# A decode step with all its gradients: turned weights as the stationary side of the output-gradient products

## The chip, the cores and the metric

The kernel runs on one core of a Trainium2 chip. The metric is the device time of one execution in microseconds (us). Five engines share the work: TensorE (PE in the profile; its weight loads are PEld), VectorE (DVE), ScalarE (ACT), GpSimd (POOL) and SyncE (SP), which issues nearly all DMAs.

## The reference

A forward pass and the gradients of all its inputs but one are wanted. B = 2 rows of width 576 are normalized to xn, and

```
out = x + A(xn) + M(xn)
A:  q = xn wq (32 heads of 128);  scores q k / sqrt(128) over 4096 cached positions (16 kv heads, 2 q heads each);
    p = softmax;  o = p v;  A = o wo
M:  g = xn w_gate, u = xn w_up (576 -> 4608);  h = g u;  M = h w_down
outputs: out, and for grad_out = dy the gradients of x, k_cache, v_cache, wq, wo, w_gate, w_up, w_down
```

All data are bf16. The caches (2 x 16 x 4096 x 128 each, 33.5 MB) are read once and their gradients, of the same size, are written once; so are the weights and theirs. The profile counts 92.48 MB read and 92.48 MB written.

The weight gradients are outer products of two rows each: of wo it is o (4096 long, called R in a group of 512) times dy; of w_down it is h (4608 long, called hb in a block of 512) times dy; of w_gate and w_up it is xn times the gradients of g and u (D in the code). The products that need dy from the left are dy wo^T (the gradient of o) and dy w_down^T (the gradient of h).

## The kernel before

**Pieces.** Attention goes in 8 groups of 4 q heads (2 kv heads), each for 2 batch rows, so 16 steps. `group_front` makes q and the gradient of o for a group, `softmax` and `dscore` the scores of a step and their gradients, `contract` (matmuls at L1378) the two context products, `head_outer` (L1226) the cache gradients as outer products, `group_back` what follows on o and q. The MLP goes in 9 blocks of 512 columns, `mlp`, loaded in pairs.

**Turning.** A product that contracts over a weight's or cache's free dimension needs it turned. DVE turns 32x32 blocks of pairs of bf16 (as fp32), in `t32` (L418), into a buffer X. So after a turn, the two elements of a pair stay side by side, and products take every second element: index e or parity in the code.

**Output-gradient products.** In `group_front` (L967) and `mlp` (L841), dy, laid out in `Wdy` with zeros around, is the stationary side (128x128) and the turned weights X the moving side, 128 columns; 18 products add up 576 rows. The result in PSUM has a batch row for each 32-block of partitions. In `group_front` it is copied to `dof`, turned on PE (L978) and copied to qd; in `mlp` it is multiplied with gs into D (L849).

**Row products of weight gradients.** `rows_outer` makes a 512x576 gradient of wo or w_down as 4 units (`rows_unit`). A unit is 8 matmuls at L675 with 32 contracted rows and a stationary side of 32 columns: for each of 2 banks, four matmuls that stand on the diagonal of the array (rows 32q, output partitions 32q). The result is evicted as 2 x 288 columns into a staging buffer, and `put` (L644) stores it.

**Evictions and buffers.** `cp` copies on ACT (L422) or DVE (L424). PSUM has three double banks `ps_o` for what is evicted to staging, and two banks `ps_m` for everything else, which a stream holds from ACQ("m") to REL("m"). 16 buffers of 1 MB ("big") hold cache tiles, turned tiles and staging; a cache load waits for a free one.

**What sets the order.** Each piece is a generator that yields what it needs (an engine with a cost, a buffer, an event). A planner (`Order`) runs when the program is built: it keeps a clock for each engine by the yielded costs, a line for the DMAs, and picks what starts first, by priorities in the table PRI and a slack for each engine; `BIAS` weighs DVE against ACT for evictions, and `AT` says after which cache load a weight load may be issued. So the order of every engine's instructions, and that of SP's DMA queue, comes from these numbers. On the chip each engine follows that order and waits for semaphores. Engines issue in order: behind a waiting instruction everything on its engine waits.

## Time and profile before

| | |
|---|---|
| time, median of 3 runs | 472.86 us (472.06 to 473.0) |
| profiled execution | 471.37 us, its span 469.6 us |
| mean granted PE clock | 0.71 |
| busy PE / PEld / DVE / ACT / POOL | 370.8 / 217.5 / 369.5 / 334.3 / 146.8 us |
| moved | 185.96 MB, 396 GB/s over the span |
| PE matmuls | 6636 |

The span runs from the first to the last instruction of the profiled execution. Busy times are of that execution; overlapping matmuls of a group count once. The strip of the profile cuts the span into 40 equal slices and gives each engine's busy tenths, the granted clock of TensorE in tenths, the share in which the DMA engines were busy, and the rate. A group's row names line, engine, operation, tiles and shape, then the busy time of the whole group, the mean duration of one instruction in ns, and the idle time of the engine before them with what ended it.

### The profile page before, as it was taken

Reading aid. Unit: us, or ns where it says so; the run is one execution under the profiler, and the core shown is the slowest. Engines: PE = TensorE matmul, PEld = TensorE weight load, DVE = VectorE, ACT = ScalarE, POOL = GpSimd, SP = SyncE. Lnnn points to the kernel's source line nnn. Section 1 sums busy time; section 2 is a strip of 40 time slices with the busy share of each in tenths; the row PEclk is TensorE's granted clock in tenths of the full one; section 3 lists DMA queues with packets and bytes.
Section 4 is the critical chain, followed back from the end, with each engine's and each line's share of the span. In section 5 each row is a group of like instructions: output and inputs, shape, how many; then the busy total and the mean of one; then the engine's idle time right before and its main releaser. Section 6 shows DMA issues by size and latency. Waiting matters only on the chain.

```text
span 469.6 us, 15459 instructions
## 1 busy us (share of the span) xinstructions
PE 370.8 (79%) x6636; PEld 217.5 (46%) x6636; DVE 369.5 (79%) x705; ACT 334.3 (71%) x507; POOL 146.8 (31%) x176
## 2 busy tenths in 40 slices
PE   0588688869887777986997669789699898998984
PEld 0455444435653352554463444564345434444453
DVE  9689878967867879688689658978867978898772
ACT  2149668867885948671798638877678678789973
POOL 3350242681330320203252264000843705325100
PEclk9978897767757668776675767956656658566977
DMA  8999999999999999999999999999999989999995
GB/s 317 404 413 403 363 390 419 409 416 421 418 416 420 399 421 406 412 415 419 399 418 404 386 418 424 408 413 342 413 416 393 424 270 416 423 413 413 424 368 176
DMA packets 40053, 185.96 MB, mean 396 GB/s; under 512 B 3496, under 2 KB 11184, under 8 KB 23600
## 3 DMA queue, kind: packets, MB, share of 16 engines
q1 hardware_dynamic: 39976, 184.96, 98.1%
q8 instruction: 52, 0.85, 0.7%
q14 instruction: 17, 0.14, 0.1%
q10 hardware_dynamic: 8, 0.00, 0.0%
HBM read 92.48 MB, written 92.48 MB: 394 GB/s over the span
## 4 chain that ended last, share of the span: by engine, by line
PE 42%; ACT 18%; DVE 18%; DMA 12%; issue 5%; POOL 2%; SPq 2%; ACTq 0%; DVEq 0%; POOLq 0%
ACT big L422 15%; DMA out_dram<-big 10%; DVE big L418 8%; PE ps_m L1378 8%; PE ps_o L1226 7%; PE ps_m L1205 7%; PE ps_o L675 4%; PE ps_m L841 3%; DVE big L424 3%; DMA big<-in_A_v_cache_dram 3%; PE ps_m L967 2%; PE ps_m L636 2%; POOL BD L1193 2%; PE ps_o L712 1%; SPq L1129 1%
## 5 line engine op out<-in xcount | busy, mean ns | idle before, releaser
L422 ACT CAST big<-ps_o 128x1024 bf16<-128x1024 f32 (+4 forms) x319 | 279.7, 950 | 40.3 <-PE ps_o L1226 18.2
L418 DVE STREAM_TRANSPOSE big<-big 128x1024 f32<-128x1024 f32 x146 | 176.1, 1223 | 5.9 <-DMA big<-in_A_v_cache_dram 3.6
L1193 POOL TENSOR_TENSOR BD<-vr,mask 128x2048 bf16<-128x2048 bf16 x32 | 115.2, 3603 | 198.8 <-ACT vr L422 122.2
L424 DVE CAST big<-ps_o 128x1024 bf16<-128x1024 f32 (+2 forms) x71 | 78.2, 1102 | 15.8 <-PE ps_o L675 5.2
L1205 PE MATMUL ps_m<-big,W 128*32 128x128 bf16 x2048 | 57.1, 274 | 5.5 <-ACT osb L422 0.7
L1226 PE MATMUL ps_o<-BD,dd 32*128 32x512 bf16 x256 | 48.8, 489 | 12.7 <-ACT big L422 9.2
L1205 PEld LDWEIGHTS <-W 128*32 128x32 bf16 x2048 | 45.4, 121 | 21.9 <-issue 18.6
L1226 PE MATMUL ps_o<-BD,pp 32*128 32x512 bf16 x256 | 42.1, 461 | 10.4 <-ACT big L422 6.7
L1170 POOL COPY W<-rep 32x16 bf16<-32x16 bf16 x128 | 24.5, 192 | 63.5 <-DVE rep L951 53.2
L418 DVE STREAM_TRANSPOSE big<-ww 128x1152 f32<-128x1152 f32 (+1 forms) x25 | 32.9, 1317 | 4.5 <-DMA out_dram<-big 3.3
L1378 PE MATMUL ps_m<-big,pp 128*32 128x512 bf16 x256 | 28.2, 536 | 1.5 <-DVE small L1330 1.2
L1378 PE MATMUL ps_m<-big,dd 128*32 128x512 bf16 x256 | 27.5, 518 | 1.5 <-DVE dd L418 0.6
L1226 PEld LDWEIGHTS <-dd 32*128 32x128 bf16 x256 | 11.8, 97 | 32.4 <-issue 24.7
L1226 PEld LDWEIGHTS <-pp 32*128 32x128 bf16 x256 | 10.4, 95 | 26.9 <-issue 22.6
L422 ACT CAST osb<-ps_m 128x512 bf16<-128x512 f32 x15 | 8.9, 590 | 15.9 <-PE ps_m L1378 12.6
L675 PE MATMUL ps_o<-dyr,R 32*32 32x288 bf16 x256 | 17.3, 402 | 2.0 <-ACT big L422 2.0
L675 PE MATMUL ps_o<-dyr,hb 32*32 32x288 bf16 x288 | 16.5, 346 | 1.1 <-ACT big L422 0.9
L967 PE MATMUL ps_m<-big,Wdy 128*128 128x128 bf16 x144 | 14.9, 285 | 3.1 <-DVE small L1283 2.0
L712 PEld LDWEIGHTS <-xnr 32*128 32x128 bf16 x368 | 12.5, 119 | 9.3 <-issue 8.6
L422 ACT CAST sp<-ps_m 128x256 bf16<-128x256 f32 x22 | 8.4, 380 | 11.2 <-PE ps_m L1213 11.0
L636 PEld LDWEIGHTS <-wm 128*32 128x32 bf16 x704 | 13.4, 115 | 6.3 <-issue 5.1
L841 PE MATMUL ps_m<-big,Wdy 128*128 128x128 bf16 x162 | 15.6, 272 | 0.6 <-DVE small L1291 0.4
(210 smaller groups left out, 481.9 us busy)
## 6 DMA issues: line engine op xcount, KB each, us to landing
out_dram<-big SPq DMA_DIRECT2D x74, 1024.0 KB, 12.1
big<-in_A_k_cache_dram SPq DMA_DIRECT2D x32, 1024.0 KB, 12.4
big<-in_A_v_cache_dram SPq DMA_DIRECT2D x32, 1024.0 KB, 12.5
out_dram<-big SPq DMA_DIRECT2D x17, 576.0 KB, 11.4
ww<-in_B_w_down_dram SPq DMA_DIRECT2D x9, 576.0 KB, 11.1
ww<-in_A_wo_dram SPq DMA_DIRECT2D x8, 576.0 KB, 11.1
ww<-in_A_wq_dram SPq DMA_DIRECT2D x8, 512.0 KB, 11.6
big<-in_B_w_gate_dram SPq DMA_DIRECT2D x4, 1024.0 KB, 13.1
```

Of the source, the lines that this page charges most:

```text
L418: nc.vector.transpose(out, in_)
L422: nc.scalar.copy(out, in_)
L424: nc.vector.tensor_copy(out=out, in_=in_)
L636: nc.tensor.matmul(dp[32 * q:32 * q + 32, :], lhsT=view(Wm[:], 0, P, 8 * pos(q, s), [[1, 32]]), rhs=view(X, 0, P, xoff(q, s), [[FS, blocks ...
L675: nc.tensor.matmul(o[32 * q:32 * q + 32, aa, 0:HD2], lhsT=view(t, 32 * q, 32, 2 * A + aa, [[4, 32]]), rhs=dyr[32 * q:32 * q + 32, k * HD2: ...
L841: nc.tensor.matmul(dh, lhsT=Wdy[:, e, 2 * k:2 * k + P], rhs=view(X[:], 0, P, 64 * k + e, [[D, FC], [2, 32]]), start=(k == 0 and e == 0), s ...
L967: nc.tensor.matmul(dp, lhsT=Wdy[:, e, 2 * k:2 * k + P], rhs=view(X[:], 0, P, 64 * k + e, [[D, GH], [2, 32]]), start=(k == 0 and e == 0), s ...
L1170: nc.gpsimd.tensor_copy(view(W_t[t][w][:], 32 * a, 32, 6 + 8 * a, [[G * WW, 4], [WW, G], [1, 2]]), view(rep_t[grp[g]["qs"]][:], 32 * a, 32 ...
L1193: nc.gpsimd.tensor_tensor(BD_t[i][:], view(vr_t[v][:], 0, P, 0, [[0, 16], [1, Dh]]), view(mask16[:], 0, P, 0, [[1, 16], [0, Dh]]), ALU.mult)
L1205: nc.tensor.matmul(sc[32 * cq:32 * cq + 32, :], lhsT=view(W[:], 0, P, (be * G + l) * WW + 6 - 4 * c2 - 2 * l, [[1, 32]]), rhs=view(X[:], 0 ...
L1226: nc.tensor.matmul(o[:, k, :], lhsT=pr2[32 * c4:32 * c4 + 32, :], rhs=BD[32 * c4:32 * c4 + 32, 8 * l + 4 * h2:8 * l + 4 * h2 + 4, :], star ...
L1378: nc.tensor.matmul(ct[32 * j:32 * j + 32, :], lhsT=view(rT, 0, P, 4 * c + 2 * l, [[1, 32]]), rhs=kv_t[kvS[s][t][l]][:, Dh * c:Dh * (c + 4) ...
```

## The change

**Output-gradient products.** The turn writes X in another order (`turn_rows`), so that 128 columns of one product lie at a step of two elements. X is now the stationary side (128x128), and dy, packed as 8 columns in `dy8`, the moving side (`dy_products`): 18 products again, with 8 moving columns each. The result has the 512 positions on partitions and in 4 columns per batch row. In `group_front` it is copied straight to qd, and `dof` with its transpose goes. In `mlp` it is copied to E, and a product of E with a rearranged identity (`unmix`) gives the gradient of h in the layout that D needs. `selx` and `unmix` serve the changed order of positions where qd is used later.

**Row products.** A unit is now 2 matmuls with 32 contracted rows and a stationary side of 128 columns, one in each of the two banks. For this hb and R hold the positions in the order c, p instead of p, c: `mlp` turns hb by DVE into hT as before (earlier now), transposes hT on PE and copies it back to hb; `group_back` builds R by 16 products with strided columns of the identity instead of 4 transposes. rT comes from a PE transpose and a copy of 8 columns instead of a DVE turn, and gT from two PE transposes and a copy of 16 columns instead of a DVE turn.

**Order.** The MLP row products are spawned before the wait for w_down instead of after D. The costs that the streams yield follow the new pieces, and the numbers in PRI, AT, BIAS and SLACK are other ones, found by a new search.

```diff
--- before.py
+++ after.py
@@ -257 +257 @@
 PRI = {
-    "turn0": [12127.5, 6592.3, 21769.7, -2605.1, ...
+    "turn0": [23153.9, 17883.7, 20715.9, 24467.2, ...
...
 AT = {
-    "wq": [-5, 7, 11, 24, 31, -18, 50, -5],
-    "wo": [-13, -2, -15, 2, 36, -14, 47, 53],
-    "mlp": [2, 16, -13, 39, 111],
+    "wq": [-20, 4, -15, 24, 28, 2, 47, -17],
+    "wo": [-20, -11, -20, 24, 36, -11, -2, -5],
+    "mlp": [2, 15, -12, 39, 86],
 }
@@ -301 +301 @@
 CLK = 1.65
-BIAS = 0.21111771427708687
-SLACK = {"PE": 0.0, "ACT": 0.11786185086953341, "DVE": 0.44815392421950667, "POOL": 1e9, "SP": 1e9}
+BIAS = 0.27538315644118333
+SLACK = {"PE": 0.0, "ACT": 0.03971586105496694, "DVE": 0.4579872161471015, "POOL": 1e9, "SP": 1e9}
 
@@ -380 +380 @@
     hT_t = [const.tile([P, FC, 32], BF16, name=f"hT{i}") for i in range(2)]
-    gT_t = [const.tile([P, 8, 32], BF16, name=f"gT{i}") for i in range(2)]
+    gT_t = [const.tile([P, 4, 2, 2], BF16, name=f"gT{i}") for i in range(2)]
     wm_t = tiles("wm", 2, [P, 35, 8])
@@ -386 +386 @@
     rep_t = [const.tile([P, 2, 4, GH * 2], BF16, name=f"rep{i}") for i in range(2)]
-    dof = const.tile([P, P], BF16, name="dof")
-    rT = const.tile([P, GH, 32], BF16, name="rT")
+    E_t = [const.tile([P, 4, 32], BF16, name=f"E{i}") for i in range(2)]
+    rT = const.tile([P, GH, 2], BF16, name="rT")
     R_t = tiles("R", 2, [P, P])
@@ -454 +454 @@
             nc.gpsimd.memset(t[r], 0.0)
-    Wdy = filled("Wdy", [P, 2, 160], BF16, 0.0)
+    dy8 = filled("dy8", [P, 2 * NB, 4, 2], BF16, 0.0)
     xnd = filled("xnd", [P, 2, P], BF16, 0.0)
@@ -459 +459 @@
 
-    for t in (*W_t[0], *W_t[1], *wm_t, *oT_t):
+    for t in (*W_t[0], *W_t[1], *wm_t, *oT_t, *E_t):
         nc.vector.memset(t[:], 0.0)
@@ -469 +469 @@
     identP = const.tile([P, P], BF16, name="identP")
-    selA = const.tile([P, 4, 4, 32], BF16, name="selA")
+    selx = const.tile([P, 4, 4, 16, 2], BF16, name="selx")
+    unmix = view(ident[:], 0, P, 0, [[1, 32], [32, 4]])
     K4 = const.tile([P, 4], FP32, name="K4")
@@ -514 +515 @@
         for be in range(4):
-            nc.vector.tensor_copy(selA[:, be], view(ident[:], 0, P, 32 * be, [[0, 4], [1, 32]]))
+            nc.vector.tensor_copy(selx[:, be], view(ident[:], 0, P, 32 * (be % 2) + 16 * (be // 2), [[0, 4], [1, 16], [64, 2]]))
         yield DVE(0.2)
@@ -547 +548 @@
         for a in range(4):
-            nc.vector.tensor_copy(
-                view(Wdy[:], 32 * a, 32, 32 * a, [[2, NB], [160, 2], [1, 2]]),
-                dyT[32 * a:32 * a + 32, :, 0:2].rearrange("p (k e) b -> p k e b", e=2))
+            nc.vector.tensor_copy(dy8[32 * a:32 * a + 32, :, a, :], dyT[32 * a:32 * a + 32, :, 0:2])
         yield SET(Edy)
@@ -668 +667 @@
 
+    def dy_products(out, X):
+        for k in range(NB):
+            for e in range(2):
+                nc.tensor.matmul(out, lhsT=view(X[:], 0, P, 2 * P * k + e, [[2, P]]),
+                                 rhs=dy8[:, 2 * k + e].rearrange("p a b -> p (a b)"),
+                                 start=(k == 0 and e == 0), stop=(k == NB - 1 and e == 1))
+
+    def turn_rows(X, w):
+        t32(pairs(X[:, 0:WB]).rearrange("p (k c i) -> p c k i", c=FC, i=32),
+            pairs(w[:]).rearrange("p (c k r) -> p c k r", c=FC, r=32))
+
     def rows_unit(j, t, st):
@@ -673 +683 @@
             for aa in range(2):
-                for q in range(4):
-                    nc.tensor.matmul(o[32 * q:32 * q + 32, aa, 0:HD2], lhsT=view(t, 32 * q, 32, 2 * A + aa, [[4, 32]]),
-                                     rhs=dyr[32 * q:32 * q + 32, k * HD2:(k + 1) * HD2], start=True, stop=True)
+                c = 2 * A + aa
+                nc.tensor.matmul(o[:, aa, 0:HD2], lhsT=t[32 * c:32 * c + 32, :],
+                                 rhs=dyr[32 * c:32 * c + 32, k * HD2:(k + 1) * HD2], start=True, stop=True)
 
@@ -679 +689 @@
             cp(e, view(st[:], 0, P, 2 * A * D + k * HD2, [[D, 2], [1, HD2]]), o[:, :, 0:HD2])
-        return mms, (0.12, 0.208), D, ev
+        return mms, (0.12, 0.052), D, ev
 
@@ -810 +820 @@
         hs = yield ACQ("hb")
-        hb, hT, gT = hb_t[hs], hT_t[hs], gT_t[hs]
-        f0 = i * FS
+        hb, hT, gT, E = hb_t[hs], hT_t[hs], gT_t[hs], E_t[hs]
         yield WAIT(Lgu, Exn, Emore, Ezero)
@@ -828 +837 @@
         nc.vector.tensor_tensor(hb[:], gs[:, 0], ug[:, 1], ALU.mult)
-        yield REL("m", m)
+        yield DVE(0.31)
+        t32(hT[:].rearrange("p c m -> p (c m)"), view(hb[:], 0, P, 0, [[1, 4], [4, 32]]))
+        hp = m_t[m][:].bitcast(BF16)[:, 4 * P:5 * P]
+        yield PE(0.053, 0.03)
+        nc.tensor.transpose(hp, hT[:].rearrange("p c m -> p (c m)"), ident[:])
+        e = yield EV(128)
+        cp(e, hb[:], hp)
+        yield REL("m", m)
+        hE = Event()
+        yield SPAWN(rows_outer(hb[:], out_8[i * FS:(i + 1) * FS, :], pr("mlp", i) + pr("wout"), hE),
+                    pr("mlp", i) + pr("wout"))
 
@@ -834 +853 @@
         yield DVE(1.37)
-        t32(pairs(X[:, 0:FC * D]), pairs(wd[:, 0:FC * D]))
-        m = yield ACQ("m")
+        turn_rows(X, wd)
+        m = yield ACQ("m")
+        dT = m_t[m][:, 2 * P:2 * P + 8]
+        yield PE(0.0, 0.47)
+        dy_products(dT, X)
+        yield REL("X", x)
+        e = yield EV(8)
+        cp(e, E[:, :, 0:2], dT.rearrange("p (a b) -> p a b", b=2))
         dh = m_t[m][:, 0:P]
-        yield PE(0.96, 0.47)
-        for k in range(NB):
-            for e in range(2):
-                nc.tensor.matmul(
-                    dh, lhsT=Wdy[:, e, 2 * k:2 * k + P], rhs=view(X[:], 0, P, 64 * k + e, [[D, FC], [2, 32]]),
-                    start=(k == 0 and e == 0), stop=(k == NB - 1 and e == 1),
-                )
-        yield REL("X", x)
+        yield PE(0.053, 0.03)
+        nc.tensor.matmul(dh, lhsT=E[:].rearrange("p a m -> p (a m)"), rhs=unmix, start=True, stop=True)
         Ds[i] = ds = yield ACQ("D")
@@ -848 +867 @@
         yield DVE(0.42)
-        nc.vector.tensor_tensor(
-            view(D2[:], 0, P, 0, [[P, 2], [4, 32], [1, 4]]), view(dh, 0, P, 0, [[0, 2], [1, 32], [32, 4]]),
-            view(gs[:], 0, P, 0, [[P, 2], [4, 32], [1, 4]]), ALU.mult)
+        nc.vector.tensor_tensor(D2[:], view(dh, 0, P, 0, [[0, 2], [1, P]]), gs[:], ALU.mult)
         yield REL("m", m)
@@ -855 +872 @@
 
-        E = [Event()]
         po = pr("mlp", i) + pr("wout")
-        yield SPAWN(rows_outer(hb[:], out_8[f0:f0 + FS, :], po, E[0]), po)
         for ks in BUNCH:
@@ -861 +876 @@
                 yield SPAWN(grads(ks, po), po)
-        yield DVE(0.31)
-        t32(hT[:].rearrange("p c m -> p (c m)"), view(hb[:], 0, P, 0, [[1, 4], [4, 32]]))
-        yield DVE(0.41)
-        t32(gT[:].rearrange("p c m -> p (c m)"), view(D2[:], 0, P, 0, [[64, 4], [1, 2], [2, 32]]))
+        ws = yield ACQ("wm")
+        m = yield ACQ("m")
+        rp, tp = m_t[m][:, 0:64], m_t[m][:].bitcast(BF16)[:, 4 * P:6 * P]
+        yield PE(0.107, 0.06)
+        for w in range(2):
+            nc.tensor.transpose(tp[:, w * P:w * P + P], D2[:, w], ident[:])
+        e = yield EV(16)
+        cp(e, gT[:], view(tp, 0, P, 0, [[32, 4], [P, 2], [1, 2]]))
         yield SET(dE[i][1])
-
-        ws = yield ACQ("wm")
-        m = yield ACQ("m")
-        rp = m_t[m][:, 0:64].rearrange("p (k b) -> p k b", b=2)
         yield PE(0.0, 0.104)
-        for a in range(4):
-            nc.tensor.matmul(rp[:, 8 * a:8 * a + 8, :], lhsT=selA[:, a].rearrange("p a i -> p (a i)"),
-                             rhs=gT[:, :, 0:2], start=True, stop=True)
+        for be in range(4):
+            nc.tensor.matmul(view(rp, 0, P, 2 * be, [[8, 8], [1, 2]]), lhsT=sel[:, be].rearrange("p a i -> p (a i)"),
+                             rhs=gT[:].rearrange("p a w b -> p (a w) b"), start=True, stop=True)
         yield from stationaries(ws, rp, 32, 0.42)
@@ -914 +929 @@
         yield SET(left[1].pop())
-        yield WAIT(*E)
+        yield WAIT(hE)
         yield REL("hb", hs)
@@ -947 +962 @@
             for be in range(4):
-                nc.tensor.matmul(rp[:, be, :], lhsT=sel[:, be].rearrange("p a i -> p (a i)"),
+                nc.tensor.matmul(rp[:, be, :], lhsT=(sel[:, be].rearrange("p a i -> p (a i)"), selx[:, be].rearrange("p a i e -> p (a i e)"))[t],
                                  rhs=qd[:, t].rearrange("p h b -> p (h b)"), start=True, stop=True)
@@ -960 +975 @@
         yield DVE(1.37)
-        t32(pairs(X[:, 0:GH * D]), pairs(wo[:, 0:GH * D]))
-        m = yield ACQ("m")
-        dp = m_t[m][:, 0:GH * 32]
-        yield PE(0.96, 0.47)
-        for k in range(NB):
-            for e in range(2):
-                nc.tensor.matmul(
-                    dp, lhsT=Wdy[:, e, 2 * k:2 * k + P], rhs=view(X[:], 0, P, 64 * k + e, [[D, GH], [2, 32]]),
-                    start=(k == 0 and e == 0), stop=(k == NB - 1 and e == 1),
-                )
+        turn_rows(X, wo)
+        m = yield ACQ("m")
+        dT = m_t[m][:, 0:8]
+        yield PE(0.0, 0.47)
+        dy_products(dT, X)
         yield REL("X", x)
-        e = yield EV(128)
-        cp(e, view(dof[:], 0, P, 0, [[1, 4], [4, 32]]), dp.rearrange("p (c i) -> p c i", c=4))
-        yield REL("m", m)
-        m = yield ACQ("m")
-        dT = m_t[m][:].bitcast(BF16)[:, 0:P]
-        yield PE(0.0, 0.1)
-        nc.tensor.transpose(dT, dof[:], ident[:])
         e = yield EV(8)
-        cp(e, qd[:, 1], view(dT, 0, P, 0, [[32, GH], [1, 2]]))
+        cp(e, qd[:, 1], dT.rearrange("p (h b) -> p h b", b=2))
         yield REL("m", m)
@@ -996 +999 @@
         m = yield ACQ("m")
-        rp = m_t[m][:].bitcast(BF16)
-        yield PE(0.0, 0.21, kind="c")
-        for t in range(2):
-            for h in range(GH):
-                nc.tensor.transpose(rp[32 * h:32 * h + 32, P * t:P * t + P], oT[:, t, h, :], ident[:])
-        for t, x in ((0, R), (1, Q)):
+        rp, qp, rq = m_t[m][:, 0:P], m_t[m][:].bitcast(BF16)[:, 2 * P:3 * P], m_t[m][:].bitcast(BF16)[:, 3 * P:4 * P]
+        yield PE(0.08, 0.3, kind="c")
+        for h in range(GH):
+            for c in range(4):
+                nc.tensor.matmul(rp[32 * c:32 * c + 32, 32 * h:32 * h + 32], lhsT=oT[:, 0, h, :],
+                                 rhs=view(ident[:], 0, P, c, [[4, 32]]), start=True, stop=True)
+        for h in range(GH):
+            nc.tensor.transpose(qp[32 * h:32 * h + 32, :], oT[:, 1, h, :], ident[:])
+        for x, t in ((R, rp), (Q, qp)):
             e = yield EV(128)
-            cp(e, x[:], rp[:, P * t:P * t + P])
+            cp(e, x[:], t)
+        yield PE(0.053, 0.03)
+        nc.tensor.transpose(rq, R[:], ident[:])
+        e = yield EV(8)
+        cp(e, rT[:], rq.rearrange("p (c m) -> p c m", m=32)[:, :, 0:2])
         yield REL("m", m)
@@ -1007 +1017 @@
         po = pr("back", g) + pr("wout")
-        yield DVE(0.31)
-        t32(rT[:].rearrange("p c m -> p (c m)"), view(R[:], 0, P, 0, [[1, 4], [4, 32]]))
         yield SPAWN(rows_outer(R[:], out_5[n0:n0 + FS, :], po, E[0]), po)
@@ -1186 +1194 @@
                                  lhsT=qr_t[grp[g]["qs"]][:, t, b, :],
-                                 rhs=ident[:], start=True, stop=True)
+                                 rhs=(ident[:], unmix)[t], start=True, stop=True)
                 e = yield EV(128)
```

## The prediction

> **What bounds the kernel now.** I read the page's strip of 40 slices first, then the stretches, the DMA queue's waits, the chain, and last the groups by shape. The strip and the queue table:
>
> ```profile
> PEclk9978897767757668776675767956656658566977
> DMA  8999999999999999999999999999999989999995
> GB/s 317 404 413 403 363 390 419 409 416 421 418 416 420 399 421 406 412 415 419 399 418 404 386 418 424 408 413 342 413 416 393 424 270 416 423 413 413 424 368 176
> ...
> q1 hardware_dynamic: 39976, 184.96, 98.1%
> ```
>
> A slice is 469.6/40 = 11.74 us. A typical undisturbed one moves 415 GB/s, and 185.96 MB at that rate take 448.1 us: the span is 21.4 us longer than its bytes. Slice by slice, (415 - rate)/415 x 11.74 us puts 2.8 us into the first slice (nothing loaded yet), 8.1 us into the last two (the drain), and a net 10.6 us between, of which the slices at 342 and 270 GB/s (from 317 and 376 us) hold 2.1 and 4.1, and those at 363 and 390 (47 to 70 us) 2.2. No edit can win more than about these 21 us, and only what starves the queue can be won. Three stretches (columns: length, busy PE, PEld, DVE, ACT, POOL with counts, granted clock, DMA share, GB/s):
>
> ```profile
> 0.00:20.00 20.00, 4.17 (x77) 2.81 (x81) 17.73 (x78) 5.22 (x9) 5.49 (x13) 1.00 0.92 350
> ...
> 340.00:360.00 20.00, 19.31 (x233) 9.16 (x231) 13.50 (x27) 16.66 (x23) 8.28 (x16) 0.57 1.02 403
> ...
> 455.00:470.00 15.00, 7.29 (x190) 5.13 (x190) 4.92 (x19) 6.40 (x10) 0.00 (x0) 0.73 0.50 177
> ```
>
> And who held SP's queue from 372 to 390 us (us in all, times, longest):
>
> ```profile
> SPq L1087 <- PE ps_m L1378: 7.8, 1, 7.8
> SPq L1087 <- DVE big L418: 5.4, 1, 5.4
> SPq L644 <- DVE big L424: 5.0, 1, 5.0
> ```
>
> In the worst stretch a cache load waited 7.8 us for PE's context products (L1378) to release its buffer, and a store 5.0 us for an eviction. Over the whole span SP waited 112.3 us for ACT's evictions (L422) and 90.6 us for DVE's (L424): the queue is fed just in time by products and evictions together. PE is 370.8 us busy, 79%, and 42% of the chain, with the edited lines on it (L675 3.9%, L841 2.7%, L967 2%). So PE matters, but only through starved stretches. The rows that the edit is priced by (busy us in all, mean ns of one):
>
> ```profile
> L1226 PE MATMUL ps_o<-BD,dd 32*128 32x512 bf16 x256 | 48.8, 489 | 12.7 <-ACT big L422 9.2 <-DVE big L424 1.3 <-POOL BD L1193 0.9
> ...
> L675 PE MATMUL ps_o<-dyr,R 32*32 32x288 bf16 x256 | 17.3, 402 | 2.0 <-ACT big L422 2.0
> L675 PE MATMUL ps_o<-dyr,hb 32*32 32x288 bf16 x288 | 16.5, 346 | 1.1 <-ACT big L422 0.9
> L841 PE MATMUL ps_m<-big,Wdy 128*128 128x128 bf16 x162 | 15.6, 272 | 0.6 <-DVE small L1291 0.4
> L967 PE MATMUL ps_m<-big,Wdy 128*128 128x128 bf16 x144 | 14.9, 285 | 3.1 <-DVE small L1283 2.0 <-DVE small L1330 0.6 <-DVE big L418 0.4
> ...
> L882 PE MATMUL ps_m<-hT,ww 128*128 128x2 bf16 x180 | 5.9, 164 | 0.2 <-DVE oT L1398 0.2
> ```
>
> **Part 1, row products.** 17 blocks (8 of R, 9 of hb) of 4 units. A unit is now 8 matmuls; busy (17.3 + 16.5)/68 = 0.50 us. It becomes two matmuls of the L1226 shape, 288 columns for 512. L1226 with both its operands is 48.8 + 42.1 us for 256 units, 0.355 us; times 288/512 that is 0.20. Saved 0.30 x 68 = 20 us of PE. If the two did not run beside each other in their two banks, 0.40 a unit, 7 us saved; if they were bound by nothing but issue, 0.10, 27 us. I take 20, since L1226 already has this shape and two banks. The evictions stay 576 columns at 651 ns (ACT) or 749 ns (DVE).
>
> **Part 2, output-gradient products.** 17 times 18 matmuls with 128 moving columns, (15.6 + 14.9)/17 = 1.79 us. The same 18 with 8 moving columns and a freshly loaded 128x128 stationary are like L882: 5.9/9 = 0.66 us for 20, so 0.59 for 18. Saved 1.2 x 17 = 20 us. The new stationary is read with a step of two elements; no row has that at 128 columns. From L882's 96 ns to L841's 144 ns median weight load it is 0.59 to 0.9 us, so 15 to 20 us saved; I keep 20, the row with the same moving width.
>
> **Part 3, what is added on PE.** Per MLP block one transpose for hb, one product with unmix for dh, two transposes for gT; per group one for rT, while that of dof goes. By dof's own row (2.0/8 = 0.25 us) 9 x (0.25 + 0.25 + 0.3) + 8 x 0.25 - 2.0 = 7.2 us. R is put together by 16 small products instead of 4 transposes: 8 transposes are 2.7/8 = 0.34 us now, 20 pairs by L882 0.66, so 8 x 0.35 = 2.8 us more. Net PE: -20 - 20 + 10 = -30 us of 371.
>
> **Part 4, DVE and ACT.** Gone: the 32x32 turns into gT (9 x 405 ns) and rT (8 x 306 ns), 6.1 us of DVE, and dof's copies (7 on ACT, 3.2 us, one on DVE). New evictions: hb 9 x 0.28 (the vr copy's row), E, gT and rT 26 x 0.17 (the qd copy's row), 6.9 us shared by both. Net -2.7 us: I take 0. The turn of a weight block keeps its 1152 elements (1361 ns) in another write order. For other orders the trace has 678 ns for 512 elements and 417 for 256, up to 1.63 ns an element: 0 to 0.5 us more, 17 times 0 to 8.8 us. I take 0, the row of the same size, and keep 8.8 for the range. The start-up fills (E for part of Wdy, selx for selA) lie where PE idles: nil, and at most 0.4 us.
>
> **The added waits.** PE's unmix product now waits for E's copy (0.17 us, but behind whatever ACT or DVE is evicting, up to 1.2 us), and behind it on PE stand all later products. In the new PE order other products lie between the two in 8 blocks of 9 (six attention outer products, 0.97 us on the chain, or four fold products, 0.25); in one block nothing does. So the cost is 0 to 9 x 1.2 = 11 us of PE; I take 0.5 us for the open block, which disappears in rounding, and keep the rest for the range. The transposes of rT and hb wait for a copy or a turn in the same way.
>
> **Part 5, what moves.** The MLP row products and their 576 KB stores no longer wait for w_down and dh; ahead of them now stand one DVE turn (291 ns), one transpose and one copy, about 1.2 us with the handoffs, during which one of the two ps_m banks stays taken. Against that the group front drops one bank turn, and its chain from turned wo to qd is shorter by 1.2 + 0.45 + 0.25 us. I set the two equal. All DMAs stay, at other places in SP's queue, since the whole order was drawn again. After the last w_down load 10.9 MB of stores are left instead of 11.9, with an out row again ahead of the last few: the drain keeps its shape.
>
> **The sum.** 30 us less PE work cannot show as 30 us; it shows where the queue starved. From 317 to 329 us six row units lie between the products that stores waited for (0.3 each, 1.8, of which I take -1.5). At the end two runs of L675 with 16 matmuls each (1.15 and 0.98 us) hold the store at 458 us: four units, -1.2. From 47 to 66 us two row units and one L967 run: -1. In the worst stretch no edited line runs; a PE that carries 8% less gets there with less backlog, and I give it half of its 4.1: -2. Together -5.7. The profiled execution took 471.37 us (1.77 beside its span), 1.49 below the median, so 471.37 - 5.7 + 1.49 = 467.2 us. A difference under 0.2% (0.9 us) is about what a measurement of this kernel can't tell from no change.
>
> **The clock.** The rows show no law in busy time: 1.00 where PE was 4.17 of 20 us busy, 0.57 where it was 19.31. At the low clock L841 takes 2.08 us, at the high one 1.21. The Trainium skill (TensorE: Matmul & The Clock Gate, Part 1) says the reverse of those rows: the gate starts throttled, and a busy window releases it. By that rule a lighter PE loses clock. The trace disagrees at both ends, so its chance is small.
>
> **Rivals.** (a) The clock falls with the dense dy products gone. A mean lower by 0.05 means 10% more of the span at half rate: 47 us x 0.79 busy x 0.7 longer = 26 us more PE, which eats the 30. Time then 472 to 473: no change. Against it: the two stretches above. 6%. (b) The queue is full 98.1% of the time and a new order starves it elsewhere by as much: 472 to 473. 6%. (c) Slower, by one mechanism: SP issues in order, so one load placed ahead of ready stores and held for a kv buffer by PE or DVE stops all behind it, as at 370 us (7.8 us waited, 4.1 lost). With two more such places, each 4.1, against -3.7 (the part of the gain that doesn't hang on the worst stretch, which stays) the time is 472.9 + 4.5 = 477.4; one more place takes all of it back. For it: the order is new everywhere and SP stood 16.5 us for L1378. Against: less PE ahead of L1378. 24%. (d) The change doesn't do what it says: the two-bank row products run one after the other, and strided weight loads are slow. Parts 1 and 2 shrink to 7 + 15 us, net 12, two fifths of the gain: 470.6. 10%. (e) Nearly all of the middle is won: -10 to -14, 459 to 463. 14%.
>
> **How the numbers follow.** My forecast (about 464 to 470) has 40%. Faster: 40 + 14 + 10 and a little of (b), 66%; same: 6 + 4 = 10%; slower: 24%. The range leaves out a little at each end: low 458 (case e), high 479 (case c, with some of DVE's 8.8 us). The likeliest sign's own range is 459 to 471.
>
> **What would show it.** Right: L675 at two matmuls a unit and under 0.25 us a unit; the dy products at 0.55 to 0.9 us a run; PE near 340 us busy; mean clock 0.68 to 0.75; fewer slices below 400 GB/s. Wrong: an SP wait of over 5 us for L1378's successor at two or more places, weight-block turns well over 1.36 us, or a PE as busy as before.

## The result, and the profile after

The changed kernel takes 473.85 us (median of 22 runs, 471.77 to 476.27). The kernel before, run as often beside it, takes 471.56 us (469.98 to 474.91), a little less than its three runs above. The ratio is 1.0042, 95% interval 1.0025 to 1.0059: slower by 2.0 us (2.3 by the two medians), where 5.7 us less were forecast. The profiled execution of after took 472.13 us, its span is 470.3 us, and its mean granted clock 0.622 against 0.710. That execution was one of its fastest, so the two spans, only 0.7 us apart, show less than the medians do.

The page of after, the rows that answer to those of before:

```profile
PE 380.9 (81%) x6360; PEld 204.7 (44%) x6360; DVE 372.9 (79%) x723; ACT 330.7 (70%) x501; POOL 146.6 (31%) x176
...
PEclk9999655665556657555665556666656665656655
DMA  8999989999999999999999999999999999999975
GB/s 297 408 406 417 419 307 416 366 414 416 425 421 335 390 413 424 425 414 422 422 418 417 375 415 350 421 420 380 417 418 423 421 423 423 424 418 338 423 310 222
...
q1 hardware_dynamic: 39976, 184.96, 97.9%
```

PE has 276 matmuls fewer and is busy 10.1 us longer. From the fifth slice on the clock's row is fives and sixes but for one seven; before, 22 of the 40 slices had a seven or more. (The nines in front are no full clock; the section on the prediction comes to that.) At 415 GB/s the shortfall is 3.3 us in the first slice, 8.4 in the last two and 10.5 between, against 2.8, 8.1 and 10.6. The hole that was deepest before (270 GB/s, from 376 us) is gone; those at 307 (59 us), 335 (141 us), 350 (282 us) and 338 GB/s (423 us) are new and cost 3.1, 2.3, 1.8 and 2.2 us.

The same stretches as before (length, busy PE, PEld, DVE, ACT, POOL with counts, granted clock, DMA share, GB/s):

```profile
0.00:20.00 20.00, 3.97 (x69) 2.60 (x73) 17.73 (x80) 5.22 (x9) 5.26 (x13) 1.00 0.92 340
...
340.00:360.00 20.00, 19.01 (x264) 8.62 (x264) 16.02 (x32) 18.01 (x24) 10.55 (x19) 0.57 1.01 421
...
455.00:470.00 15.00, 10.93 (x170) 7.39 (x165) 6.86 (x18) 7.54 (x10) 0.00 (x0) 0.50 0.70 261
```

In the first two, PE's busy time and the clock are nearly as they were. In the last one the clock is 0.50, where it was 0.73.

Groups of PE in after (busy us in all, mean ns of one). L1213 is the score product, L1234 the outer product of the caches' gradients, L1386 the context product: the same instructions in the same number as L1205, L1226 and L1378 of before. L685 is the row product, L671 the dy product:

```profile
L1213 PE MATMUL ps_m<-big,W 128*32 128x128 bf16 x2048 | 62.9, 295 | 5.4 <-DVE vr L424 1.0 <-DVE qd L424 0.8 <-DVE qd L952 0.8
L1234 PE MATMUL ps_o<-BD,dd 32*128 32x512 bf16 x256 | 53.6, 519 | 11.1 <-ACT big L422 10.7 <-DVE big L424 0.3
L1234 PE MATMUL ps_o<-BD,pp 32*128 32x512 bf16 x256 | 50.4, 571 | 8.8 <-ACT big L422 4.9 <-POOL BD L1201 3.2
L1386 PE MATMUL ps_m<-big,pp 128*32 128x512 bf16 x256 | 32.8, 619 | 2.4 <-DVE small L1338 1.3 <-DVE pp L418 0.5 <-ACT vr L422 0.4
L1386 PE MATMUL ps_m<-big,dd 128*32 128x512 bf16 x256 | 31.1, 587 | 3.1 <-DVE dd L418 2.0 <-DVE oT L1406 0.3 <-DVE sp L424 0.3
...
L685 PE MATMUL ps_o<-dyr,R 32*128 32x288 bf16 x64 | 11.0, 388 | 1.2 <-ACT big L422 0.8
L685 PE MATMUL ps_o<-dyr,hb 32*128 32x288 bf16 x72 | 11.0, 412 | 1.3 <-ACT big L422 0.8 <-DVE big L424 0.3
L671 PE MATMUL ps_m<-dy,big 128*128 128x8 bf16 x306 | 10.7, 168 | 3.4 <-DVE small L1291 0.8 <-DVE small L1299 0.6 <-DVE big L418 0.5
```

The edited lines shrank: row products from 33.8 to 22.0 us, dy products from 30.5 to 10.7. The five attention groups, in which nothing was edited, grew from 203.7 to 230.8 us; the four of them that the lines above did not show were these:

```profile
L1205 PE MATMUL ps_m<-big,W 128*32 128x128 bf16 x2048 | 57.1, 274 | 5.5 <-ACT osb L422 0.7 <-issue 0.7 <-POOL W L1170 0.7
...
L1226 PE MATMUL ps_o<-BD,pp 32*128 32x512 bf16 x256 | 42.1, 461 | 10.4 <-ACT big L422 6.7 <-POOL BD L1193 2.0 <-DVE big L424 0.7
L1378 PE MATMUL ps_m<-big,pp 128*32 128x512 bf16 x256 | 28.2, 536 | 1.5 <-DVE small L1330 1.2 <-ACT sp L422 0.3
L1378 PE MATMUL ps_m<-big,dd 128*32 128x512 bf16 x256 | 27.5, 518 | 1.5 <-DVE dd L418 0.6 <-DVE small L1283 0.5 <-DVE wm L629 0.2
```

What SP's queue waited for in after, first from 56 to 72 us, then from 280 to 294 us, the longest wait of each (us, times, longest):

```profile
SPq L1095 <- PE ps_m L1386: 6.4, 1, 6.4
```

```profile
SPq L1095 <- PE ps_m L1386: 8.4, 1, 8.4
```

A cache load stands in the queue until the context products release its buffer, and with it all that SP has behind it: two waits of over 5 us, where before had one. The holes at 141 and 423 us have no such wait. From 139 to 156 us SP waited longest for evictions by DVE (5.8 us in 2 waits), and from 418 to 434 us no wait was longer than 1.8 us.

### The profile page after: what moved, and what is told of

Read it like the earlier page. It is cut to its first block, busy times and chain, and to the rows that moved or that the text cites. A ratio compares the mean times of both kernels' runs of the same rounds, so it can differ in the third digit from the quotient of the medians.

```text
span 470.3 us, 14943 instructions
## 1 busy us (share of the span) xinstructions
PE 380.9 (81%) x6360; PEld 204.7 (44%) x6360; DVE 372.9 (79%) x723; ACT 330.7 (70%) x501; POOL 146.6 (31%) x176
## 4 chain that ended last, share of the span: by engine, by line
PE 48%; ACT 19%; DVE 16%; issue 8%; DMA 5%; POOL 4%; ACTq 0%; DVEq 0%; POOLq 0%
ACT big L422 16%; PE ps_m L1386 10%; PE ps_o L1234 9%; PE ps_m L1213 9%; DVE big L418 8%; POOL BD L1201 3%; DMA out_dram<-big 3%; PE ps_m L635 2%; PE ps_o L685 2%; DMA gu<-in_B_w_gate_dram 2%; DVE big L424 2%; PE ps_o L722 1%; PE ps_m L832 1%; PE ps_m L1336 1%; PE ps_m L671 1%
## 5 line engine op out<-in xcount | busy, mean ns | idle before, releaser
L424 DVE CAST big<-ps_o 128x1024 bf16<-128x1024 f32 (+1 forms) x71 | 77.5, 1092 | 14.0 <-PE ps_o L1234 5.5
L1213 PE MATMUL ps_m<-big,W 128*32 128x128 bf16 x2048 | 62.9, 295 | 5.4 <-DVE vr L424 1.0
L1234 PE MATMUL ps_o<-BD,dd 32*128 32x512 bf16 x256 | 53.6, 519 | 11.1 <-ACT big L422 10.7
L1213 PEld LDWEIGHTS <-W 128*32 128x32 bf16 x2048 | 50.0, 131 | 23.3 <-issue 21.3
L1234 PE MATMUL ps_o<-BD,pp 32*128 32x512 bf16 x256 | 50.4, 571 | 8.8 <-ACT big L422 4.9
L1386 PE MATMUL ps_m<-big,pp 128*32 128x512 bf16 x256 | 32.8, 619 | 2.4 <-DVE small L1338 1.3
L1386 PE MATMUL ps_m<-big,dd 128*32 128x512 bf16 x256 | 31.1, 587 | 3.1 <-DVE dd L418 2.0
L1234 PEld LDWEIGHTS <-dd 32*128 32x128 bf16 x256 | 12.3, 99 | 33.6 <-issue 28.4
L1234 PEld LDWEIGHTS <-pp 32*128 32x128 bf16 x256 | 9.9, 100 | 29.6 <-issue 25.5
L635 PEld LDWEIGHTS <-wm 128*32 128x32 bf16 x704 | 14.7, 123 | 4.8 <-issue 4.6
L1396 ACT ACTIVATE osb<-ps_m 128x512 bf16<-128x512 f32 x14 | 8.4, 600 | 11.9 <-PE ps_m L1386 10.3
L635 PE MATMUL ps_m<-big,wm 128*32 128x128 bf16 (+1 forms) x416 | 14.8, 304 | 0.3 <-DVE small L1338 0.2
L1287 ACT COPY sp<-small 1x128 f32<-1x128 f32 x16 | 4.7, 293 | 14.7 <-DVE small L1285 14.7
## 6 DMA issues: line engine op xcount, KB each, us to landing
ww<-in_A_wq_dram SPq DMA_DIRECT2D x8, 512.0 KB, 10.5
```

Of the source, the lines that this page charges most:

```text
L424: nc.vector.tensor_copy(out=out, in_=in_)
L635: nc.tensor.matmul(dp[32 * q:32 * q + 32, :], lhsT=view(Wm[:], 0, P, 8 * pos(q, s), [[1, 32]]), rhs=view(X, 0, P, xoff(q, s), [[FS, blocks ...
L1213: nc.tensor.matmul(sc[32 * cq:32 * cq + 32, :], lhsT=view(W[:], 0, P, (be * G + l) * WW + 6 - 4 * c2 - 2 * l, [[1, 32]]), rhs=view(X[:], 0 ...
L1234: nc.tensor.matmul(o[:, k, :], lhsT=pr2[32 * c4:32 * c4 + 32, :], rhs=BD[32 * c4:32 * c4 + 32, 8 * l + 4 * h2:8 * l + 4 * h2 + 4, :], star ...
L1386: nc.tensor.matmul(ct[32 * j:32 * j + 32, :], lhsT=view(rT, 0, P, 4 * c + 2 * l, [[1, 32]]), rhs=kv_t[kvS[s][t][l]][:, Dh * c:Dh * (c + 4) ...
L1396: nc.scalar.activation(ob, cs, AF.Copy, scale=SCALE)
```

## The experiments

Theory A says that the clock falls with the work taken off PE and takes the gain back. B: the new order starves the queue, whatever the clock. C: the lighter pieces are worth time in a fixed order, and each set of numbers (PRI, AT, BIAS, SLACK) fits the pieces it was searched for. D: the order is dearer by itself. E: the added pieces and their waits cost it. Ratios are to the kernel before, with 95% intervals.

**The order of after, its pieces made heavier or divided.** In e1 the dy products move 128 columns again, in e2 the row unit is cut in eight, in e3 both; e4 has after's pieces and before's numbers.

```diff
 e1  -  rhs=dy8[:, 2 * k + e].rearrange("p a b -> p (a b)"),
     +  rhs=dy8[:, 2 * k + e:2 * k + e + 16].rearrange("p j a b -> p (j a b)"),
 e2  -  nc.tensor.matmul(o[:, aa, 0:HD2], lhsT=t[32 * c:32 * c + 32, :], ...)
     +  for q in range(4):
     +      nc.tensor.matmul(o[32 * q:32 * q + 32, aa, 0:HD2], lhsT=t[32 * c:32 * c + 32, 32 * q:32 * q + 32], ...)
```

> The kernel after, in the same order of instructions on every engine, with one thing changed: the 18 output-gradient products move 128 columns again in place of 8 (the 120 extra columns are not used), 36,720 columns more over the 17 runs. Theory A (the granted clock follows the columns that TensorE streams, and the change took too many away): the mean clock rises above the 0.61 to 0.685 of the changed kernel's 22 runs, by a quarter of the lost 0.07 if columns count alone (36,720 of 154,224 lost), to nearly 0.71 if it is the full 128x128 array that counts; the time falls by 0 to 1 us although the products themselves take longer. Theory B (the new order of the DMA queue starves it, the clock does not matter): time as the changed kernel's, ratio 1.002 to 1.006 or slower, by up to the 1.2 us a run that the products cost.

> The kernel after, in the same order, with a row unit cut into 8 matmuls of 32x32 (four side by side in the columns of the array for each of the two banks) in place of 2 of 32x128: same output, same multiplications, 117,504 columns more streamed. Theory A, counting columns: the clock rises by three quarters of the loss, to about 0.69; counting multiplications: it stays at 0.64. Theory B: time 1.004 or slower, whatever the clock does.

> Both of the former together: the changed kernel's order and pieces with the matmul work of the kernel before. Theory A: clock back to 0.70 to 0.72, and the time at or under the kernel before (ratio 0.998 to 1.001). Theory B: clock back, time still 1.004 or more, since the order is what it was.

> The changed kernel's pieces planned with the priorities, weight gates, bias and slacks of the kernel before. Theory A: the clock is low here too (0.62 to 0.66), as the matmul work is the changed kernel's, and the time is 1.00 to 1.01. Theory B: the time comes back to the kernel before's (0.995 to 1.001), if the numbers suit these pieces as well; numbers that were searched for other pieces may also lose 1 to 3% by themselves.

| | ratio | median us | clock, median of its runs |
|---|---|---|---|
| e1 | 1.0263 (1.0225 to 1.0301) | 482.79 | 0.661 |
| e2 | 1.0090 (1.0054 to 1.0127) | 475.61 | 0.645 |
| e3 | 1.0302 (1.0267 to 1.0337) | 485.75 | 0.661 |
| e4 | 1.0351 (1.0319 to 1.0383) | 487.64 | 0.626 |
| before, beside them | 1 | 471.1 | 0.70 to 0.71 |
| after | 1.0042 (1.0025 to 1.0059) | 473.85 | 0.643 |

The dy products of e1:

```profile
L671 PE MATMUL ps_m<-dy,big 128*128 128x128 bf16 x306 | 34.0, 302 | 3.3 <-DVE small L1291 0.8 <-DVE small L1299 0.6 <-DVE big L418 0.5
```

With 34.0/17 = 2.0 us a run for 0.63 the clock comes part of the way back, and the time goes up by 2.2%: in after's order, giving PE denser work to hold its clock is a loss. It costs more than PE's time: the whole PE is busy 384.5 us for 380.9, the kernel takes 9 us more, and the shortfall between the first and the last two slices grows from 10.5 to 19.1 us. Theory A had the time fall, so it missed here; its clock is the one that A gave for a count of columns alone. e2 was meant as the dearer unit and wasn't one: its rows stay 21.3 us. Its clock stayed (0.645 for 0.643), where a count of columns would have given 0.69 and a count of multiplications 0.64. So neither count alone fits both runs. It is 0.5% slower than after by the point values, and the intervals overlap. e3 has the multiplications and the columns of before, and A expected 0.70 to 0.72 and the time of before: it got 0.661 and 3.0% more. So the amount of work alone does not give the clock back; where the row tiles stand counts too, as g2 shows below. e4 carries the most: after's pieces in the order that before's numbers give them take 3.5% more than before and 3.1% more than after. Its clock is low as A said, but A and B both missed its time. So these numbers and these pieces belong together, and none of the four runs tells what the pieces alone are worth.

**The order of before, its pieces made lighter.** In f1 17 of the 18 matmuls of a dy run move 8 columns, in f2 the row unit is two matmuls of 32x128, in f3 both. f4 has before's pieces and after's numbers.

```diff
 f1  +  last = k == NB - 1 and e == 1
     -  dh, lhsT=Wdy[:, e, 2 * k:2 * k + P], rhs=view(X[:], 0, P, 64 * k + e, [[D, FC], [2, 32]]),
     +  dh if last else dh[:, 0:8], lhsT=Wdy[:, e, 2 * k:2 * k + P],
     +  rhs=view(X[:], 0, P, 64 * k + e, [[D, FC], [2, 32 if last else 2]]),
 f2  -  for q in range(4):
     -      nc.tensor.matmul(o[32 * q:32 * q + 32, aa, 0:HD2], lhsT=view(t, 32 * q, 32, 2 * A + aa, [[4, 32]]), ...)
     +  c = 2 * A + aa
     +  nc.tensor.matmul(o[:, aa, 0:HD2], lhsT=t[32 * c:32 * c + 32, :], ...)
```

> The kernel before, same order everywhere; 17 of the 18 matmuls of each output-gradient product move 8 columns in place of 128 (left out: most of the sums, so the gradients that need dy wo^T and dy w_down^T are not formed). Theory C (the lighter products are worth time at a fixed order, and what was lost lies in the new order): 0.985 to 0.995 of the kernel before, as the same 120 columns cost 1.9% in the changed kernel's order. Theory A (the clock takes back what the lighter products give): clock 0.65 to 0.68, time 0.998 to 1.004.

> The kernel before, same order; a row unit is 2 matmuls of 32x128 in place of 8 of 32x32 (left out: the right order of rows in the gradients of wo and w_down; every element is still computed and stored). Theory C: 0.990 to 0.998, from 12 us less PE work. Theory A: the clock falls to 0.65 to 0.68, time 0.998 to 1.004.

> Both of the former in the kernel before's order, with what both leave out. It is the lightening without the added transposes and copies and without the new order. Theory C: 0.975 to 0.990. Theory A: clock 0.62 to 0.65 as in the changed kernel, unchanged products as long as there, time 0.998 to 1.006.

> The kernel before's pieces planned with the changed kernel's priorities, gates, bias and slacks. Theory C: numbers fit the pieces that they were searched for, so this loses 1.5 to 4%, as the opposite exchange lost 3.5%. Theory A: the clock is 0.70 to 0.72, as the work is the kernel before's, and the time 1.00 to 1.01.

| | ratio | median us | clock, median of its runs |
|---|---|---|---|
| f1 | 0.9961 (0.9944 to 0.9977) | 469.96 | 0.671 |
| f2 | 0.9962 (0.9942 to 0.9982) | 469.71 | 0.675 |
| f3 | 0.9936 (0.9922 to 0.9949) | 468.58 | 0.643 |
| f4 | 1.0252 (1.0229 to 1.0276) | 483.38 | 0.699 |

f1 and f2 each win 0.4%, f1 less than C forecast, with clocks as A said. f3 is the heart of it: the order of before on every engine, with lighter row units and dy runs in their old places, and nothing added. The page of f3, and its groups (L1209, L1230 and L1382 are the attention products, L675 the rows, L842 and L970 the dy products):

```profile
PE 366.0 (78%) x6228; PEld 201.4 (43%) x6228; DVE 368.8 (79%) x705; ACT 333.5 (71%) x507; POOL 146.8 (31%) x176
...
PEclk9996556576555668756655765755655676665655
...
GB/s 311 406 413 412 414 377 395 394 407 420 388 418 421 401 416 421 423 418 421 415 416 400 391 413 423 408 414 367 412 421 413 423 325 421 421 404 371 425 368 171
```

```profile
L1209 PE MATMUL ps_m<-big,W 128*32 128x128 bf16 x2048 | 60.9, 288 | 6.0 <-DVE hb L828 1.4 <-DVE big L418 0.9 <-ACT osb L422 0.7
L1230 PE MATMUL ps_o<-BD,dd 32*128 32x512 bf16 x256 | 52.4, 520 | 11.8 <-ACT big L422 8.6 <-DVE big L424 1.2 <-DVE small L1334 0.4
L1230 PE MATMUL ps_o<-BD,pp 32*128 32x512 bf16 x256 | 47.1, 518 | 8.5 <-ACT big L422 5.5 <-POOL BD L1197 2.1 <-DVE qd L939 0.3
L1382 PE MATMUL ps_m<-big,pp 128*32 128x512 bf16 x256 | 32.7, 601 | 3.5 <-DVE pp L418 1.6 <-DVE small L1334 1.1 <-ACT big L422 0.5
L1382 PE MATMUL ps_m<-big,dd 128*32 128x512 bf16 x256 | 29.1, 552 | 1.1 <-DVE small L1287 0.5 <-DVE dd L418 0.4
...
L675 PE MATMUL ps_o<-dyr,hb 32*128 32x288 bf16 x72 | 10.9, 396 | 1.7 <-ACT big L422 1.5
L675 PE MATMUL ps_o<-dyr,R 32*128 32x288 bf16 x64 | 10.5, 410 | 5.4 <-ACT big L422 5.2
...
L842 PE MATMUL ps_m<-big,Wdy 128*128 128x8 bf16 x153 | 5.4, 169 | 0.4 <-DVE small L1295 0.4
L970 PE MATMUL ps_m<-big,Wdy 128*128 128x8 bf16 x136 | 4.8, 169 | 2.8 <-DVE small L1287 1.7 <-DVE big L418 1.1
L842 PE MATMUL ps_m<-big,Wdy 128*128 128x128 bf16 x9 | 2.4, 262 | 0.0
L970 PE MATMUL ps_m<-big,Wdy 128*128 128x128 bf16 x8 | 2.1, 262 | 0.0
```

The rows lose 33.8 - 21.4 = 12.4 us and the dy products 30.5 - 14.7 = 15.8 us, together 28.2. The attention groups grow by 222.2 - 203.7 = 18.5 us, and the rest of PE's groups by the other 10: all matmul groups added up are 431.2 us before and 431.9 in f3. PE's busy time as a whole falls by 4.8 us only, 370.8 to 366.0, and the kernel gains 3.0 us (0.64%), between what A and C had forecast. What A says happened, yet not to the end: a small gain is left, so C's first half holds too. f4 settles its second half: before's pieces in the order from after's numbers lose 2.5%.

That it is the clock which lengthens the attention products, and not something else that stands beside them, can be read from the clock records of the traces. Sorted by the clock at which a product starts, a score product adds 21.0 ns to the group's busy time at the full clock and 32.5 at the half clock in before, 21.3 and 32.4 in f3, 22.3 and 32.4 in after; in the other four groups the difference is at most 13%, either way, wherever more than four products start at that clock. What differs is how many start at the full clock: 42% of all attention products in before, 23% in f3, 15% in after. An estimate from before's times at each clock and these shares gives 219 us for f3's 222.2 and 227 for after's 230.8.

**What the new order and the added pieces cost.** g1 keeps after's numbers and light pieces and takes the added operations out; g2 is after with the old diagonal row unit; g3 is before with two-matmul rows whose result lies in another order of rows, put right by a store with rows of 1,152 bytes instead of 4,608: a complete version with half of the change.

```diff
 g1  -  nc.tensor.transpose(hp, hT[:].rearrange("p c m -> p (c m)"), ident[:])
     -  cp(e, hb[:], hp)
     -  cp(e, E[:, :, 0:2], dT.rearrange("p (a b) -> p a b", b=2))
     -  nc.tensor.matmul(dh, lhsT=E[:].rearrange("p a m -> p (a m)"), rhs=unmix, start=True, stop=True)
     -  nc.tensor.transpose(tp[:, w * P:w * P + P], D2[:, w], ident[:])
     -  nc.tensor.transpose(rq, R[:], ident[:])
     (and R by 4 transposes instead of 16 products)
 g2  -  nc.tensor.matmul(o[:, aa, 0:HD2], lhsT=t[32 * c:32 * c + 32, :], ...)
     +  for q in range(4):
     +      nc.tensor.matmul(o[32 * q:32 * q + 32, aa, 0:HD2], lhsT=view(t, 32 * q, 32, 2 * A + aa, [[4, 32]]), ...)
 g3  (f2's edit, and)
     -  put([dst.rearrange("(p c) n -> p (c n)", c=FC)], [st[:, 0:FC * D]], ...)
     +  put([dst.rearrange("(c p) n -> p c n", p=P)], [st[:, 0:FC * D].rearrange("p (c n) -> p c n", n=D)], ...)
```

> The kernel after in its own order, with the pieces that it added taken out: no transpose and copy of hb, no copy to E and no unmix product, no transposes for gT and rT (their copies read D and R instead), R by 4 transposes instead of 16 products. Left out by that: the right order of rows in the gradients of wo and w_down, and the sums that need the gradients of h and o from them. PE has about 10 us less to do than in the kernel after. Theory D (the new order by itself costs what f3 had won): 1.002 to 1.005, as the kernel after. Theory E (the added pieces and their waits cost it): 0.993 to 0.998, as f3. The clock 0.62 to 0.66 by either, since the heavy products stay out.

> The kernel after in its own order, with the row unit of the kernel before: 8 matmuls of 32x32 on the diagonal, four row groups at once (left out: the right order of rows in the gradients of wo and w_down). e2 had the same 8 matmuls of 32x32, but four to one row group, and its clock stayed at 0.645. If what holds the clock is how long and over how many rows TensorE streams, the clock rises to 0.66 to 0.68 as f2 fell by 0.03 without these units, and the unit takes 0.45 to 0.55 us; if it is only the multiplications, it stays at 0.645. Time 1.005 to 1.012 by theory A or C, since more PE work in this order has cost time each time.

> A complete variant of the kernel before, in its order: row units of 2 matmuls of 32x128 without any added transpose, by storing the rows of the gradients of wo and w_down in their own order, in packets of 1,152 bytes instead of 4,608 (17 stores of 576 KB). If f2's gain holds and the smaller packets cost nothing: 0.996. If a store of small packets takes a tenth longer (10 MB, 24 us at 415 GB/s): 1.000 to 1.003.

| | ratio | median us | clock, median of its runs |
|---|---|---|---|
| g1 | 0.9994 (0.9978 to 1.0011) | 471.53 | 0.649 |
| g2 | 1.0133 (1.0108 to 1.0159) | 477.44 | 0.686 |
| g3 | 1.0028 (1.0016 to 1.0039) | 473.02 | 0.671 |

g1 lies between f3 and after, and its interval touches neither's; it is also between what D and E had forecast. From f3 to g1 the pieces are nearly the same (g1 has besides lost some DVE turns and the copies of `dof`, starts its MLP row products earlier, and its dy products take 10.7 us for 14.7) and the order is the new one: +0.58%, 2.7 us. From g1 to after the order of what both have is the same and the added operations come in: +0.48%, 2.3 us. With -0.64% (-3.0 us) for the lighter pieces these are the three steps from before to after, +0.42% in all. They add up by construction, and taken in another order the steps could have other sizes. The long waits go with the order: over the whole span SP waited for the context products 16.5 us in 7 waits before, 10.7 in 4 in f3, 34.0 in 11 in after, and in g1, without any added piece:

```profile
SPq L1086 <- PE ps_m L1377: 23.6, 8, 6.3
```

The shortfall between the first and the last two slices goes the same way from f3 to g1: 10.6 us before, 8.6 in f3, 11.0 in g1, 10.5 in after. (After's profiled run was one of its fastest, so what the added operations cost does not show in it.) That D has these waits as its mechanism is read from these profiles and not tested by itself.

g2's rows, on the diagonal of the array, and e2's, with all four on one row group:

```profile
L685 PE MATMUL ps_o<-dyr,hb 32*32 32x288 bf16 x288 | 20.1, 411 | 1.1 <-ACT big L422 1.1
L685 PE MATMUL ps_o<-dyr,R 32*32 32x288 bf16 x256 | 16.8, 389 | 0.5 <-ACT big L422 0.3
```

```profile
L686 PE MATMUL ps_o<-dyr,R 32*32 32x288 bf16 x256 | 10.8, 374 | 1.4 <-ACT big L422 0.9
...
L686 PE MATMUL ps_o<-dyr,hb 32*32 32x288 bf16 x288 | 10.5, 385 | 1.6 <-ACT big L422 1.0 <-DVE big L424 0.4
```

36.9 us against 21.3 for the same number of 32x32 matmuls with the same columns. So the gain in the row products does not come from fewer instructions. The traces show where it comes from: in e2 all eight matmuls of a unit start within 23 ns, while on the diagonal the four of the second bank, which use the same four tiles of the array again, start from 223 ns after the first four on at the half clock (from 123 at the full). A unit takes 440 ns in e2 and 673 in g2 at the half clock. (g2's stationary side is also read at a step of four elements, and its loads take 121 ns for 93; this was not varied by itself.) g2's clock rose to 0.686, a little more than was expected if the time and the rows that TensorE streams over count; yet it is 0.9% slower than after. g3 loses 0.66% to f2, its twin with long store rows, and ends slower than before. None of the complete versions beats before.

## Why the prediction was wrong, point by point

**Three steps failed.** Between the forecast -5.7 us and the measured +2.0 lie 7.7 us. The lighter pieces in the old order gave 3.0 us and not 5.7 (2.7 missing); the new order, which the sum took at nothing, cost 2.7; the added operations, which had no term of their own in it, cost 2.3. The first alone would have left the sign right.

**The clock, and rival (a): the step that halved the gain.** The fall of the clock was given 6%, because "the rows show no law in busy time" and the trace was said to disagree with a clock that starts low. One of the two rows was misread. The profile prints 1.00 wherever a trace has no clock record, and before's first record is at 23.3 us, after's at 43.1 us. The dy run of before that lies ahead of it is this one:

```profile
20.49 2.10 PE L967 MATMUL ps_m<-big,Wdy 128*128 128x128 bf16 x18
```

Such a run takes 2.08 us at the low clock and 1.21 at the high one, so here the clock was low, where the strip has a nine. In all thirteen traces the products ahead of the first record are as far apart as at the half clock (27 ns from start to start for those with 2 moving columns, for 25 at the full clock; 107 for 57 in the six traces that have a run of 128 moving columns there). "1.00 where PE was 4.17 of 20 us busy" was no measurement, and every mean clock in this document is too high by that start, most where the first record comes late.

The profiled runs in order of their clock with the start counted at half speed, and the five attention groups added up, which have the same instructions in all of them:

| profiled run | clock, start at half | clock as shown | attention groups, us | pieces | numbers |
|---|---|---|---|---|---|
| before | 0.685 | 0.710 | 203.7 | heavy | before's |
| f4 | 0.677 | 0.703 | 208.5 | heavy | after's |
| f1 | 0.649 | 0.684 | 212.5 | light dy | before's |
| g2 | 0.647 | 0.679 | 215.6 | light dy | after's |
| g3 | 0.645 | 0.671 | 210.7 | light rows | before's |
| f2 | 0.643 | 0.667 | 210.2 | light rows | before's |
| e1 | 0.639 | 0.663 | 219.8 | light rows | after's |
| e3 | 0.627 | 0.652 | 219.4 | light rows | after's |
| g1 | 0.609 | 0.655 | 225.0 | light | after's |
| f3 | 0.599 | 0.633 | 222.2 | light | before's |
| e2 | 0.593 | 0.632 | 227.3 | light | after's |
| e4 | 0.584 | 0.630 | 228.5 | light | before's |
| after | 0.576 | 0.622 | 230.8 | light | after's |

Two pairs are enough: with the numbers exchanged, heavy pieces keep 0.70 (as shown) and light pieces 0.63, so the pieces set the clock far more than the order does. And the lower it is, the longer the same products take, with exceptions of up to 5 us. The Trainium skill (TensorE: Matmul & The Clock Gate, Part 1) says that the throttled state is the default and activity releases it; I wrote that the trace disagreed, and set it aside. These runs agree with it: the clock is low at the start, and it falls with the work taken out. My second mistake was to take the busy share of a 20 us stretch for activity: a PE that is busy 19.31 of 20 us with narrow or quarter-height products can have a clock of 0.57. Rival (a) put a fall of 0.05 at 26 us of PE and no change in time; in f3 it fell by 0.06 (medians) to 0.08 (profiles), and of 28.2 us less work PE's busy time kept 4.8. Its time of 472 to 473 did not come from the clock alone, as f3 is still 3.0 us faster than before. Nor does the mean clock order single runs: of after's 22, the one with the highest (0.685) was the slowest (476.27 us).

**Part 1, row products.** Right in kind, mis-sized: 22.0/68 = 0.32 us a unit for the 0.20 forecast, 12 us saved for 20. The 0.20 was scaled from a row at the old clock; the same row, L1234, now gives (53.6 + 50.4)/256 x 288/512 = 0.23. And a product does not shrink with its columns: one with 288 (L685) takes 401 ns on average and one with 512 (L1234) takes 545, a ratio of 0.73 and not 0.56. With that the row gives 0.30.

**Part 2, dy products.** Right: 10.7/17 = 0.63 us a run against 0.59, and 20 us saved. The stationary side read at a step of two elements cost nothing that could be seen: its loads take 106 ns and its products 168, for 104 and 169 in f3, where the stationary side is contiguous.

**Part 3 and the added waits.** Forecast as 10 us of PE off the path, with 0.5 us of the waits counted. PE's busy time is 380.9 in after and 364.1 in g1, and the time 2.3 us more. That these operations reach the end at all was not in the sum. The waits that it looked for were small: PE sat idle 0.5 us in all before the nine unmix products (L864) and 2.5 before the nine transposes of hT (L842). The split between their work and their waits was not tried by itself.

**Part 4, DVE and ACT.** Right: DVE +3.4 us, ACT -3.6. The weight turns take 1358 ns, for 1361, so the bound of 8.8 us wasn't used.

**Part 5, what moves.** It set the earlier row products against the shorter group front ("I set the two equal") and had no term for an order drawn anew. That costs 2.7 us. What the profile of after shows looks like rival (c)'s mechanism, in two places as it said, 6.4 and 8.4 us waited; they lost 3.1 and 1.8 us of transfer for the 4.1 that each was given, two other new holes have no such wait, and the worst place of before went. So its sign was right, by a mechanism that is seen and not tested, and its 477.4 was too high. Two long waits were also named beforehand as a sign of being wrong, as was a PE as busy as before. f4 and e4 show why an order cannot be taken at nothing: the same pieces under the other set of numbers lost 2.5 and 3.1%.

**The sum, -5.7.** f3 tests its sites without the order. At 376 us the hole shrank from 4.1 to 2.5 us (2 forecast). At 317 us, 367 for 342 GB/s, 0.7 (1.5 forecast). From 47 to 70 us 1.1 was won (1 forecast), but the two slices behind give 1.1 back, at 395 and 394 for 419 and 409 GB/s. At the end nothing (1.2 forecast): 8.2 us for 8.1, with a clock near 0.5 there. In all the span is 1.9 us shorter, and the time 3.0 us by the ratio, for 5.7. Two of the four sites are there at about half their size or better, one is given back and one missing. It fits that the PE that was to reach them earlier was busy 4.8 us less and not 30.

**What stays open.** What the 28 us would be worth with the clock held at 0.70 could not be tried: the edits that brought part of it back (e1 to 0.661, g2 to 0.686) also put the work back. So it is shown that the fall of the clock took PE's saving, and argued that this is why 3.0 us came of 5.7.

## What to carry to other kernels

A clock of 1.00 at the start of a strip may be no record at all: time a product there that is also found later at both clocks. Before counting a lighter PE as saved time, look at what the removed products did for the clock: dense full-array matmuls may pay for a part of themselves by speeding up all the others, so compare the sum over all PE groups, not the edited rows. Price an order that is drawn anew as a term with a sign of its own: test the pieces in the old order first, then the order, since here each was about as large as the gain. And in an order tuned for short runs (after's), lengthening one again can cost far more than the PE time it adds, as e1 shows (9 us for 3.6).

## What the runs showed of the hardware

- The records hold the granted clock in windows of 3.41 us or whole multiples of it, at full or at half speed. Ahead of the first record (22.9 to 44.9 us into the thirteen traces) the profile shows 1.00, while the products there run as at half speed.
- Over all thirteen traces, the multiplications that PE finished in one window tell the next window's clock in about 91% of 1,802 cases: full from about 2,900 columns through the full 128x128 array on (rows x columns of the stationary side x moving columns / 16,384; an estimate from the traces' matmul records, fp32 counted four times). Always saying half would be right in 74%, and PE's busy share at its best cut in 79%. A dy run of before is 18 x 128 = 2,304 such columns, four fifths of that; a run of after is 144. In the last stretch of after above PE is busy 10.93 of 15 us at 0.50.
- That count isn't the whole law: e2 and g2 have the same multiplications in their row units, and the diagonal ones of g2, which take 1.7 times as long, hold a clock of 0.686 for e2's 0.645. And f2 and e1, whose multiplications are at least before's, have 0.675 and 0.661 for 0.70.
- Four 32x32 matmuls on one row group took as long together as one 32x128 matmul of the same columns (21.3 us in e2 and 22.0 in after for all units); on the diagonal, where both banks use the same four tiles, 36.9 us.
- Storing the same bytes in rows of 1,152 instead of 4,608 bytes cost 0.66% (g3 against f2).
